# One-hot tiles of a token listing, laid out with the position innermost instead of the column

## The chip, the cores and the metric

The kernel runs on one core of a Trainium2 chip. TensorE (PE) multiplies matrices, with weight loads shown apart as PEld; VectorE (DVE) and ScalarE (ACT) work on rows of the 128 partitions; GpSimd (POOL) does some elementwise work and issues indirect DMAs; SyncE (SP) issues the other DMAs. The metric is the device time of one execution in microseconds.

## What is computed

```python
x = fft(fft(x, axis=1), axis=2).real            # 8 x 3072 x 256 -> 24576 tokens of 256
h = x @ w_in                                    # 256 -> 2048
x = where(h > 0, h, exp(min(h, 0)) - 1) @ w_out # 2048 -> 256
logits = x @ w_gate                             # 8 experts, room for 3072 tokens each
for idx in argsort(-logits.flatten()):          # greedy, best logit first
    tok, e = idx // 8, idx % 8
    if assigned[tok] < 0 and counts[e] < 3072:
        assigned[tok] = e; counts[e] += 1
for e in range(8):
    out[assigned == e] = relu(x[assigned == e] @ w1[e]) @ w2[e]
```

## The kernel before

The first part, `moe1` (up to about 2000 us), does the transforms and the dense layer, and leaves the tokens in DRAM and the logits in the tile L. The second part, `moe2`, is where the change lies. It makes three kinds of work and interleaves them:

- `select(i)` finds which expert fills up next and at which logit (a bisection of 32 steps, each with a count on DVE and ACT and a small matmul), and gives every token of that expert a rank from 0 to 3071 in the tile ui, with 192 columns (token 128 j + p stands in column j of partition p).
- `listing(i)` turns the ranks into a list of token numbers. It splits a rank into rb, its last seven bits, and qb, the rest (0 to 23). The columns are taken 16 at a time, in 12 chunks. For a chunk DVE builds `oh`, for each of the 16 columns the one-hot of rb (128 wide, L479), and `oq`, 48 wide: the one-hot of qb scaled by the partition number in its upper half (L473, scaled on ACT at L475), and by the column number in its lower half (L474). `place` (L452) then multiplies, for each of the 16 columns, oh as the weights with oq as 48 moving columns, 16 matmuls into one PSUM tile. DVE adds that tile to pj (L457, the first chunk L459). For expert 0, before any expert runs, oh and oq live in other buffers (yh, yl, hh.., hl..), L474 runs on POOL, and all chunks add up in one PSUM tile. At the end idx (L498) is computed from pj and the tokens are fetched by indirect DMA (yg, L522).
- `expert(i)` runs six groups of 512 tokens. In each, eight steps of six 512-column matmuls (L553) into the three buffers of hps, each followed by a relu on ACT (hh, L565) and the rounding rest on DVE (hl, L571), which frees the buffer; then transposes of the next group (`turn`, L531, L534, L535), then 96 matmuls of 256 columns (L594 to L596).

The interleaving is fixed when the program is built: a small clock model in the kernel counts estimated time on PE, DVE and ACT (`pe`, `dve`, `act`) and puts a piece of `listing` or `select` between two expert matmuls when DVE's estimated time is not too far ahead. A chunk is counted there as 750 + 1300 ns of DVE and no time of PE, in the kernel before and in the changed one. On the chip each engine then works through its queue in that order. So that the lists are ready in time, `listing(i + 1)` runs during `expert(i)`; there are 84 chunks in seven such bursts, and 12 chunks of expert 0 in a start-up before the first expert. While the listing runs, POOL also computes the rounding rests of the next expert's weights (w1l at L434, w2l at L440), two-input subtractions of 1024 elements.

Of the kernel before, what the change touches and what calls it, by code (L numbers as in the profile page):

```python
# [11 lines left out]
BF16 = mybir.dt.bfloat16  # L12
I32 = mybir.dt.int32
U16 = mybir.dt.uint16
AF = mybir.ActivationFunctionType
OP = mybir.AluOpType
# [145 lines left out]
def moe2(tc, yd, R, w1, w2, out):  # L162
    nc = tc.nc
    L, kh, kl, hm, mx, eq = (R[n] for n in ("L", "kh", "kl", "hm", "mx", "eq"))
    identf, identb, jp = R["identf"], R["identb"], R["jp"]
    iof, pci, pe8, es2, esn = (R[n] for n in ("iof", "pci", "pe8", "es2", "esn"))
    from contextlib import ExitStack
    with ExitStack() as ctx:
        con = ctx.enter_context(tc.tile_pool(name="con2", bufs=1))
        ctx.enter_context(nc.allow_low_precision(reason="counts up to 2048 are exact in float16"))  # L170
        rt = ctx.enter_context(tc.tile_pool(name="rt", bufs=1))
        wp = ctx.enter_context(tc.tile_pool(name="wp", bufs=1))
        ex = ctx.enter_context(tc.tile_pool(name="ex", bufs=2))
# [4 lines left out]
        def rps(shape, dtype=F32):  # L178
            return psum.tile(shape, dtype, name="rps")

        pcol = con.tile([128, 1], F32, name="pcol")
        tri = con.tile([128, 128], BF16, name="tri")
        onesb = con.tile([128, NJ], BF16, name="onesb")
        io16 = con.tile([128, 128, 16], BF16, name="io16")
        jb = con.tile([128, NJ], BF16, name="jb")
        trij = con.tile([96, 2, NJ], BF16, name="trij")
        pc96 = con.tile([128, 1], F32, name="pc96")
# [8 lines left out]
        def consts():  # L196
            nc.gpsimd.memset(asg, 0.0)
            nc.vector.tensor_scalar(tri, jp, 0.0, None, op0=OP.is_gt)
            nc.vector.memset(onesb, 1.0)
            yield  # L200
            nc.vector.tensor_copy(pcol, pci)
            nc.vector.tensor_copy(jb, iof)
            yield
            nc.vector.tensor_scalar(pc96, pcol, 96.0, None, op0=OP.add)
            nc.vector.tensor_scalar(em8, iof[:, 0:E], -8.0, None, op0=OP.add)
            yield
            nc.vector.tensor_scalar(pd8i, pci, 3, None, op0=OP.logical_shift_right)
            nc.vector.tensor_scalar(pe7, pe8, -8.0, None, op0=OP.add)
            nc.vector.tensor_copy(pd8, pd8i)
            yield  # L210
            nc.vector.tensor_scalar(wsel, iof[:, 0:16], pd8, 100.0, op0=OP.not_equal, op1=OP.mult)
            nc.vector.tensor_scalar(wsel, wsel, pe7, None, op0=OP.add)
            for h in range(2):
                yield
                nc.vector.tensor_scalar(trij[:, h], iof[0:96], (pcol, pc96)[h][0:96], None, op0=OP.is_gt)
            for h in range(4):
                yield
                hs = slice(32 * h, 32 * h + 32)
                nc.vector.tensor_copy(io16[:, hs], iof[:, hs].unsqueeze(2).to_broadcast([128, 32, 16]))

        setup = consts()
        NT = NC * 128

        def small(name, w=1, dtype=F32, bufs=2):
            return rt.tile([128, w], dtype, name=name, bufs=bufs)
# [20 lines left out]
        def act(d):  # L246
            ck.act = max(ck.act, ck.pe + 200) + d

        def dve(d, after=0):
            ck.dve = max(ck.dve, ck.pe + 200, after) + d  # L250
# [3 lines left out]
        def after():  # L254
            return max(ck.dve, ck.act) + AF0
# [157 lines left out]
        def listing(i):  # L413
            while i not in st:
                yield None
            rb, qb, wix = (st[i][n] for n in ("rb", "qb", "wix"))
            wr = [wp.tile([128, 2 * FE], F32, name="wr%d" % a) for a in range(2)]
            for a, src in enumerate((w1.rearrange("e (p c) f -> (e p) (c f)", c=2),
                                     w2.rearrange("e (p c) d -> (e p) (c d)", c=8))):
                nc.gpsimd.indirect_dma_start(out=wr[a], out_offset=None, in_=src,  # L420
                                             in_offset=bass.IndirectOffsetOnAxis(ap=wix[:, 0:1], axis=0))
            fetched = ck.pe
            pj = small("pj", 48)
            prev = None
            while now[0] < i - 1:
                yield None
            wsp = [wp.tile([128, 2 * FE], F32R, name=n, bufs=2) for n in ("w1h", "w1l", "w2h", "w2l")]

            def split():
                for c in range(2):  # L430
                    rv = wr[0].rearrange("p (c f k) -> p c k f", c=2, k=8)[:, c]
                    hv, lv = (t.rearrange("p (c k f) -> p c k f", c=2, k=8)[:, c] for t in wsp[0:2])
                    nc.scalar.activation(hv, rv, AF.Copy)
                    (nc.gpsimd if i else nc.vector).tensor_tensor(lv, rv, hv, op=OP.subtract)  # L434
                    act(950)
                    yield after()
                for c in range(2):
                    ws = slice(1024 * c, 1024 * c + 1024)
                    nc.scalar.activation(wsp[2][:, ws], wr[1][:, ws], AF.Copy)
                    nc.gpsimd.tensor_tensor(wsp[3][:, ws], wr[1][:, ws], wsp[2][:, ws], op=OP.subtract)  # L440
                    act(950)
                    yield after()

            parts = split()

            if i == 0:
                pl0 = psum.tile([128, 48], F32, name="acc20")

            def place(c, oh, oq):
                pl = rps([128, 48]) if i else pl0  # L450
                for j in range(16):
                    nc.tensor.matmul(pl, oh[:, :, j], oq[:, :, j], start=j == 0 and (i > 0 or c == 0),  # L452
                                     stop=j == 15 and (i > 0 or c == NC - 1))
                if i == 0:
                    return
                if c:
                    nc.vector.tensor_tensor(pj, pl, pj, op=OP.add)  # L457
                else:
                    nc.vector.tensor_copy(pj, pl)  # L459

            for c in range(NC):
                js = slice(16 * c, 16 * c + 16)
                if i:
                    oh = rt.tile([128, 128, 16], BF16, name="oh", bufs=2)
                    oq = rt.tile([128, 48, 16], BF16, name="oq", bufs=2)
                else:
                    oh = ex.tile([128, 128, 16], BF16, name=("yh", "yl")[c % 2])
                    oq = ex.tile([128, 48, 16], BF16, name="h%s%d" % ("hl"[c % 2], c // 2), bufs=1)

                def row(a, n):  # L470
                    return a[:, js].unsqueeze(1).to_broadcast([128, n, 16])

                nc.vector.tensor_tensor(oq[:, 24:48], io16[:, 0:24], row(qb, 24), op=OP.is_equal)  # L473
                (nc.vector if i > 0 else nc.gpsimd).tensor_tensor(oq[:, 0:24], oq[:, 24:48], row(jb, 24), op=OP.mult)  # L474
                nc.scalar.activation(oq[:, 24:48], oq[:, 24:48], AF.Copy, scale=pcol)  # L475
                dve(750)
                act(450)
                yield 0
                nc.vector.tensor_tensor(oh, io16, row(rb, 128), op=OP.is_equal)  # L479
                if prev:  # L480
                    place(*prev)
                prev = (c, oh, oq)
                dve(1300)
                if ck.pe > fetched + WAIT:
                    next(parts, None)
                yield after()
            place(*prev)
            while ck.pe < fetched + WAIT and i and not draining[0]:
                yield None
            if i:  # L490
                yield from parts
            st[i]["listed"] = True
            while now[0] < i - 1:
                yield None
            idx = small("idx", 24, I32)
            if i == 0:
                nc.vector.tensor_copy(pj, pl0)
            nc.vector.scalar_tensor_tensor(idx, pj[:, 0:24], 128.0, pj[:, 24:48], op0=OP.mult, op1=OP.add)  # L498
            plan[i] = dict(idx=idx, wr=wr)
            plan[i]["w"] = wsp  # L500
            if i:
                ahead()
            else:
                fetch(*queue.pop(0))
                out_y[0] += 1
            dve(100)
            yield after()
            yield from parts
# [4 lines left out]
        def ahead():  # L513
            while queue and out_y[0] < 3 and queue[0][0] in plan:
                fetch(*queue.pop(0))
                out_y[0] += 1
# [116 lines left out]

        sel_s = Stream(select, E)
        lst_s = Stream(listing, E)

        def ready(i):
# [655 lines left out]
```

## Time and profile before

| What | Value |
|---|---|
| Median of 3 runs | 3498.51 us (3496.53 to 3498.52) |
| The profiled execution, its own time | 3501.21 us |
| Its span, first to last instruction | 3499.4 us |
| PE busy over the span | 3343.9 us (96%) |
| DVE busy over the span | 2637.1 us (75%) |
| Mean granted TensorE clock | 0.974 of full speed |

Busy time is the time in which an engine works on an instruction; a busy PE may still be slowed, since a matmul's own duration overlaps that of the next. What a matmul costs is read from the distance between starts.

### The profile page before, as it was taken

What the parts mean: (1) busy time and instruction counts of PE and PEld (TensorE: products, weight loads), DVE (VectorE), ACT (ScalarE), POOL (GpSimd) and SP (SyncE); (2) the same over time, 40 slices, a digit from 0 to 9 for tenths busy, and PEclk for the clock granted to TensorE, in tenths of its full rate; (3) what the DMA queues carried; (4) which work ended last, traced back from release to release, by engine and by line L of the source; (5) the groups of instructions that cost most, each with busy time, mean ns of one, the idle gap of its engine ahead of it and who ended that gap; (6) DMA issues with size and microseconds to landing.
All of it is one profiled execution on the core that took longest, in us unless ns stands there. A gap on an engine that the chain in (4) does not pass through costs nothing.

```text
span 3499.4 us, 62303 instructions
## 1 busy us (share of the span) xinstructions
PE 3343.9 (96%) x25464; PEld 3121.6 (89%) x25464; DVE 2637.1 (75%) x4924; ACT 2253.9 (64%) x3029; POOL 649.7 (19%) x836
## 2 busy tenths in 40 slices
PE   7999999999999999999999838999999999999998
PEld 4999999999999999999999827888798888888997
DVE  7887888888878888888878887677677777767432
ACT  3787777778778777777777636454546464545332
POOL 5000000000000000000000033333343434343332
PEclk9999999999999999999999958999999999999999
DMA  7112121121121121211100001111111111111110
GB/s 196 35 45 52 41 45 31 51 42 40 32 45 51 34 44 40 42 46 36 37 13 13 19 25 43 49 48 51 40 55 44 53 43 60 63 36 61 40 46 31
DMA packets 97078, 159.30 MB, mean 46 GB/s; under 512 B 18464, under 2 KB 68632, under 8 KB 94616
## 3 DMA queue, kind: packets, MB, share of 16 engines
q1 hardware_dynamic: 67016, 64.05, 7.4%
q0 software_dynamic: 24576, 80.21, 7.4%
q10 hardware_dynamic: 5200, 11.05, 1.1%
q8 instruction: 200, 3.28, 0.4%
q14 instruction: 86, 0.70, 0.1%
HBM read 91.78 MB, written 63.47 MB: 44 GB/s over the span
## 4 chain that ended last, share of the span: by engine, by line
PE 85%; DVE 6%; ACT 4%; issue 2%; DMA 1%; POOL 0%; another core or an unknown queue 0%; ACTq 0%; DVEq 0%; POOLq 0%
PE hps L553 14%; PE acc L1113 11%; PE acc L1112 11%; PE acc L1114 11%; PE pq L1059 5%; PE pq L1061 5%; PE pq L1060 5%; PE acc L594 4%; PE acc L595 4%; PE acc L596 4%; PE rps L452 3%; PE pq L1063 3%; ACT junk L289 3%; PE pq L786 2%; PE pq L865 1%
## 5 line engine op out<-in xcount | busy, mean ns | idle before, releaser
L1114 PE MATMUL acc<-woh,gl 128*128 128x264 f32 x3072 | 872.8, 284 | 1.4 <-DVE gl L1099 1.4
L1113 PE MATMUL acc<-wol,gh 128*128 128x264 f32 x3072 | 874.0, 285 | 0.0
L1112 PE MATMUL acc<-woh,gh 128*128 128x264 f32 x3072 | 873.0, 284 | 1.0 <-DVE wol L1033 1.0
L1114 PEld LDWEIGHTS acc<-woh,gl 128*128 128x128 f32 x3072 | 578.0, 188 | 1.9 <-DVE gl L1099 1.8
L1112 PEld LDWEIGHTS acc<-woh,gh 128*128 128x128 f32 x3072 | 578.5, 188 | 1.2 <-issue 1.2
L1113 PEld LDWEIGHTS acc<-wol,gh 128*128 128x128 f32 x3072 | 577.6, 188 | 0.0
L1082 ACT ACTIVATE e<-h 128x1024 f32<-128x1024 f32 x384 | 407.7, 1062 | 158.8 <-DVE h L1076 158.8
L1075 DVE TENSOR_TENSOR h<-pq,qs 128x512 f32<-128x512 f32 x384 | 265.5, 691 | 284.9 <-ACT qs L1069 284.0
L1099 DVE TENSOR_TENSOR gl<-g,gh 128x1024 fp32r<-128x1024 f32 x384 | 467.5, 1217 | 1.6 <-ACT gh L1094 1.6
L1089 DVE SCALAR_TENSOR_TENSOR g<-e,h 128x1024 f32<-128x1024 f32 x384 | 466.9, 1216 | 0.1
L594 PE MATMUL acc<-w2h,hh 128*128 128x256 f32 x1536 | 456.6, 297 | 0.0
L595 PE MATMUL acc<-w2l,hh 128*128 128x256 f32 x1536 | 436.2, 284 | 0.0
L596 PE MATMUL acc<-w2h,hl 128*128 128x256 f32 x1536 | 435.6, 284 | 0.0
L571 DVE SCALAR_TENSOR_TENSOR hl<-hps,hh 128x512 fp32r<-128x512 f32 x384 | 262.7, 688 | 217.1 <-ACT hh L565 202.7
L1084 ACT ACTIVATE e<-e 128x1024 f32<-128x1024 f32 x384 | 407.3, 1061 | 10.7
L1094 ACT ACTIVATE gh<-g 128x1024 fp32r<-128x1024 f32 x384 | 403.6, 1051 | 2.1 <-PE acc L1113 2.1
L1069 ACT ACTIVATE qs<-pq 128x512 f32<-128x512 f32 x384 | 229.8, 598 | 208.2 <-PE pq L1063 204.3
L565 ACT ACTIVATE hh<-hps 128x512 fp32r<-128x512 f32 x384 | 226.5, 593 | 198.8 <-PE hps L553 157.6
L604 POOL DMA_INDIRECT out<-osb,yg x192 | 201.9, 1052 | 619.5 <-ACT osb L601 587.2
L553 PE MATMUL hps<-yh,w1h 128*128 128x512 f32 x768 | 312.7, 407 | 2.0 <-DVE hl L571 1.8
L553 PE MATMUL hps<-yh,w1l 128*128 128x512 f32 x768 | 303.1, 395 | 0.0
L553 PE MATMUL hps<-yl,w1h 128*128 128x512 f32 x768 | 301.9, 393 | 0.0
(318 smaller groups left out, 7477.8 us busy)
## 6 DMA issues: line engine op xcount, KB each, us to landing
yd<-ysb SPq DMA_DIRECT2D x48, 514.0 KB
zd<-zev SPq DMA_DIRECT2D x30, 385.5 KB
xa<-x SPq DMA_DIRECT2D x28, 384.0 KB
zt<-zd SPq DMA_DIRECT2D x16, 193.5 KB
xa<-w_out ACTq DMA_DIRECT2D x6, 512.0 KB
zt<-zd SPq DMA_DIRECT2D x32, 96.0 KB
yg<-yd,idx POOLq DMA_INDIRECT x192
out<-osb,yg POOLq DMA_INDIRECT x192
```

What stands on the lines that cost most here:

```text
L553: nc.tensor.matmul(ps, w[:, ws], v[:, c], start=c + k == 0, stop=c + k == 3)
L594: nc.tensor.matmul(acc[t // 2][:, t % 2], hh[:, ts], w2h[:, fs], start=f == 0, stop=False)
L595: nc.tensor.matmul(acc[t // 2][:, t % 2], hh[:, ts], w2l[:, fs], start=False, stop=False)
L596: nc.tensor.matmul(acc[t // 2][:, t % 2], hl[:, ts], w2h[:, fs], start=False, stop=f == 7)
L1082: nc.scalar.activation(e, st["h"], AF.Relu, scale=-1.0)
L1084: nc.scalar.activation(st["e"], st["e"], AF.Exp, scale=-1.0)
L1089: nc.vector.scalar_tensor_tensor(g, st["e"], -1.0, st["h"], op0=OP.add, op1=OP.max)
L1094: nc.scalar.activation(st["gh"], st["g"], AF.Copy)
L1099: nc.vector.tensor_tensor(st["gl"], st["g"], st["gh"], op=OP.subtract)
L1112: nc.tensor.matmul(o, st["gh"][:, i, ts], woh(c), start=c == 0, stop=False)
L1113: nc.tensor.matmul(o, st["gh"][:, i, ts], wol(c), start=False, stop=False)
L1114: nc.tensor.matmul(o, st["gl"][:, i, ts], woh(c), start=False, stop=c == 15)
```

## The change

All one-hot tiles are turned: where the column index of a chunk (16) was the innermost dimension, the position (128 or 48) now is. So `oh[:, j]` and `oq[:, j]`, which a matmul reads, are 128 and 48 neighbouring elements, where before they lay 16 elements apart. On the DVE side, `row` now spreads each rank over the innermost dimension (a step of zero there), where before it repeated a row of 16 ranks. The constant io16 is turned in the same way. The counts of elements stay.

```diff
-        io16 = con.tile([128, 128, 16], BF16, name="io16")
+        io16 = con.tile([128, 16, 128], BF16, name="io16")
...
-                hs = slice(32 * h, 32 * h + 32)
-                nc.vector.tensor_copy(io16[:, hs], iof[:, hs].unsqueeze(2).to_broadcast([128, 32, 16]))
+                hs = slice(4 * h, 4 * h + 4)
+                nc.vector.tensor_copy(io16[:, hs], iof[:, 0:128].unsqueeze(1).to_broadcast([128, 4, 128]))
...
-                    nc.tensor.matmul(pl, oh[:, :, j], oq[:, :, j], start=j == 0 and (i > 0 or c == 0),
+                    nc.tensor.matmul(pl, oh[:, j], oq[:, j], start=j == 0 and (i > 0 or c == 0),
...
-                    oh = rt.tile([128, 128, 16], BF16, name="oh", bufs=2)
-                    oq = rt.tile([128, 48, 16], BF16, name="oq", bufs=2)
+                    oh = rt.tile([128, 16, 128], BF16, name="oh", bufs=2)
+                    oq = rt.tile([128, 16, 48], BF16, name="oq", bufs=2)
...
-                    return a[:, js].unsqueeze(1).to_broadcast([128, n, 16])
-
-                nc.vector.tensor_tensor(oq[:, 24:48], io16[:, 0:24], row(qb, 24), op=OP.is_equal)
-                (nc.vector if i > 0 else nc.gpsimd).tensor_tensor(oq[:, 0:24], oq[:, 24:48], row(jb, 24), op=OP.mult)
-                nc.scalar.activation(oq[:, 24:48], oq[:, 24:48], AF.Copy, scale=pcol)
+                    return a[:, js].unsqueeze(2).to_broadcast([128, 16, n])
+
+                nc.vector.tensor_tensor(oq[:, :, 24:48], io16[:, :, 0:24], row(qb, 24), op=OP.is_equal)
+                (nc.vector if i > 0 else nc.gpsimd).tensor_tensor(oq[:, :, 0:24], oq[:, :, 24:48], row(jb, 24), op=OP.mult)
+                nc.scalar.activation(oq[:, :, 24:48], oq[:, :, 24:48], AF.Copy, scale=pcol)
```

No instruction is added, removed or moved: every engine's queue has the same instructions in the same order as before; only the shapes and steps of L219, L452, L473, L474, L475 and L479 differ.

## Rows read from the trace of the kernel before

**Rows 1.** The page: busy us of each engine; the chain that ended last.
```profile
PE 3343.9 (96%) x25464; PEld 3121.6 (89%) x25464; DVE 2637.1 (75%) x4924; ACT 2253.9 (64%) x3029; POOL 649.7 (19%) x836
...
PE 85%; DVE 6%; ACT 4%; issue 2%; DMA 1%; POOL 0%; another core or an unknown queue 0%; ACTq 0%; DVEq 0%; POOLq 0%
```

**Rows 2.** Timeline of PE, one placement; start us, duration us, what.
```profile
3264.42 1.73 PE L452 MATMUL rps<-oq,oh 128*128 128x48 bf16 x16
3265.94 0.36 PE L594 MATMUL acc<-w2h,hh 128*128 128x256 f32 x1
```

**Rows 3.** Timeline of PE, twelve matmuls with contiguous bf16 operands.
```profile
2378.97 0.44 PE L342 MATMUL rps<-wb,gm 128*128 128x16 bf16 x12
2379.27 0.47 PE L553 MATMUL hps<-yh,w1h 128*128 128x512 f32 x1
```

**Rows 4.** Timeline of DVE, one chunk between two placements.
```profile
3266.32 0.35 DVE L473 TENSOR_TENSOR oq<-io,qb 128x384 bf16<-128x384 bf16 x1
3266.70 0.36 DVE L474 TENSOR_TENSOR oq<-oq,jb 128x384 bf16<-128x384 bf16 x1
3266.98 1.22 DVE L479 TENSOR_TENSOR oh<-io,rb 128x2048 bf16<-128x2048 bf16 x1
3270.63 0.21 DVE L457 TENSOR_TENSOR pj<-rps,pj 128x48 f32<-128x48 f32 x1 [2.43 <-PE rps L452]
```

**Rows 5.** Instructions of lines 409, 405, 264 and 219: ns min/median/max, first and last start.
```profile
L409 DVE TENSOR_TENSOR asg<-asg,u x8: 357/357/360, 2102.3 to 3231.5; 128x192 f32<-128x192 f32 x8
L405 DVE TENSOR_TENSOR L<-L,cc x7: 1748/1750/1751, 2276.5 to 3218.2; 128x1536 f32<-128x1536 f32 x7
L264 DVE TENSOR_TENSOR eq<-L,mx x7: 1757/1758/3852, 2108.6 to 3089.9; 128x1536 bf16<-128x1536 f32 x7
L219 DVE CAST io<-iof x4: 417/417/418, 2014.5 to 2020.1; 128x512 bf16<-128x512 f32 x4
```

**Rows 6.** Start-up, all engines: one cycle of two chunks.
```profile
2094.96 1.21 DVE L479 TENSOR_TENSOR yh<-io,rb 128x2048 bf16<-128x2048 bf16 x1
2095.12 1.85 POOL L474 TENSOR_TENSOR hh<-hh,jb 128x384 bf16<-128x384 bf16 x1 [0.29 <-DVE hh L473]
...
2096.10 1.07 DVE L473 TENSOR_TENSOR hl<-io,qb 128x384 bf16<-128x384 bf16 x1
...
2097.10 1.21 DVE L479 TENSOR_TENSOR yl<-io,rb 128x2048 bf16<-128x2048 bf16 x1
```

**Rows 7.** Busy time by stretch, from a burst's first placement to its last: PE, PEld, DVE, ACT, POOL.
```profile
2220.00:2276.00 56.00, 54.83 (x415) 49.63 (x413) 34.76 (x57) 22.39 (x32) 19.85 (x19) 0.97 0.06 21
...
3221.00:3279.00 58.00, 58.00 (x464) 53.88 (x463) 38.25 (x60) 23.30 (x32) 28.24 (x27) 1.00 0.20 67
sum 443.00, PE 439.67 PEld 400.98 DVE 305.76 ACT 183.58 POOL 185.94; mean PE 62.81 PEld 57.28 DVE 43.68 ACT 26.23 POOL 26.56
```

**Rows 8.** The same stretches, L479 alone: busy us and count, clock, DMA share.
```profile
2220.00:2276.00 56.00, 13.58 (x12) 0.97 0.06 21
...
3221.00:3279.00 58.00, 13.39 (x11) 1.00 0.20 67
```

**Rows 9.** Timeline, two subtractions on POOL and DVE beside them.
```profile
3239.24 3.06 POOL L434 TENSOR_TENSOR w1l<-wr,w1h 128x1024 fp32r<-128x1024 f32 x1
...
3240.32 4.55 DVE L473 TENSOR_TENSOR oq<-io,qb 128x384 bf16<-128x384 bf16 x1
...
3242.25 2.40 POOL L440 TENSOR_TENSOR w2l<-wr,w2h 128x1024 fp32r<-128x1024 f32 x1
```

**Rows 10.** Groups by line from 2114 us on: count, busy us, mean ns, idle before.
```profile
L479 DVE TENSOR_TENSOR oh<-io,rb 128x2048 bf16<-128x2048 bf16 x84 | 106.6, 1269 | 0.0
...
L473 DVE TENSOR_TENSOR oq<-io,qb 128x384 bf16<-128x384 bf16 x84 | 54.7, 651 | 0.2
...
L474 DVE TENSOR_TENSOR oq<-oq,jb 128x384 bf16<-128x384 bf16 x84 | 32.9, 391 | 2.9
```

More of the change, by code (lines that the diff above doesn't have):

```diff
@@ L463, in listing @@
                 if i:
-                    oh = rt.tile([128, 128, 16], BF16, name="oh", bufs=2)
-                    oq = rt.tile([128, 48, 16], BF16, name="oq", bufs=2)
-                else:
-                    oh = ex.tile([128, 128, 16], BF16, name=("yh", "yl")[c % 2])
-                    oq = ex.tile([128, 48, 16], BF16, name="h%s%d" % ("hl"[c % 2], c // 2), bufs=1)
+                    oh = rt.tile([128, 16, 128], BF16, name="oh", bufs=2)
+                    oq = rt.tile([128, 16, 48], BF16, name="oq", bufs=2)
+                else:
+                    oh = ex.tile([128, 16, 128], BF16, name=("yh", "yl")[c % 2])
+                    oq = ex.tile([128, 16, 48], BF16, name="h%s%d" % ("hl"[c % 2], c // 2), bufs=1)
                 def row(a, n):
-                    return a[:, js].unsqueeze(1).to_broadcast([128, n, 16])
-                nc.vector.tensor_tensor(oq[:, 24:48], io16[:, 0:24], row(qb, 24), op=OP.is_equal)
-                (nc.vector if i > 0 else nc.gpsimd).tensor_tensor(oq[:, 0:24], oq[:, 24:48], row(jb, 24), op=OP.mult)
-                nc.scalar.activation(oq[:, 24:48], oq[:, 24:48], AF.Copy, scale=pcol)
+                    return a[:, js].unsqueeze(2).to_broadcast([128, 16, n])
+                nc.vector.tensor_tensor(oq[:, :, 24:48], io16[:, :, 0:24], row(qb, 24), op=OP.is_equal)
+                (nc.vector if i > 0 else nc.gpsimd).tensor_tensor(oq[:, :, 0:24], oq[:, :, 24:48], row(jb, 24), op=OP.mult)
+                nc.scalar.activation(oq[:, :, 24:48], oq[:, :, 24:48], AF.Copy, scale=pcol)
                 dve(750)
```

## The prediction

> **What bounds the kernel now.** I read the page first. PE is busy 96% of the span and carries 85% of the chain that ended last, DVE only 75% [rows 1]. That reads as if whatever shortens PE shortens the kernel. But the change touches PE in seven bursts, so the share that matters is the one inside them. The view by stretch gives it: from a burst's first placement to its last the seven make 443 us, in which PE is busy 439.7 and DVE 305.8, 69% [rows 7]. PE is the bound there, with 137 us of DVE idle beside it.
>
> Then the timelines. A placement of 16 matmuls starts at 3264.42 and the next matmul starts at 3265.94: 1.52 us of PE, 95 ns each [rows 2]. The twelve matmuls of L342, whose bf16 weights and moving columns are contiguous, take 2379.27 - 2378.97 = 0.30 us, 25 ns each [rows 3]. On DVE a chunk is 0.35 + 0.36 + 1.22 us and the addition to pj [rows 4].
>
> The start-up is another case: PE waits there, and DVE and POOL take turns. L479 runs from 2094.96 to 2096.17; L474 on POOL, started at 2095.12, ends only at 2096.97, 0.8 us after L479; the next L473, 0.35 us elsewhere, takes 1.07 and ends just after that. A chunk takes 2097.10 - 2094.96 = 2.14 us, all of it in this ring [rows 6].
>
> **PE's side of the change.** With both operands contiguous I take the rate of L342 and a little for 48 instead of 16 columns: 16 x 28 ns = 0.45 us a placement. Gain 1.52 - 0.45 = 1.07 us, times 84 = 90 us of PE. The bounds are 0 (if the distance of elements is not what costs) and 16 x 25 ns, a gain of 94 us.
>
> **DVE's side.** L479 does 2048 elements in 1.22 us. L405, two fp32 inputs, needs 1.75 us for 1536, L409 0.36 us for 192: 1.04 ns an element over a fixed part [rows 5]. So L479 now goes at two elements in the time of one there. The bf16 operands it reads and writes are all neighbours; with the change the second input stands still along the innermost dimension. No row has bf16 operands of that kind. Lower bound: the rate stays, 1.22 us. Upper bound: one element at a time, 1.75 + 512 x 0.00104 = 2.28 us. For the lower speaks L219, which reads a value that stands still 16 times and yet does 512 elements in 417 ns; it has one input. For the upper speaks L264, which has two inputs, one of them standing still, and takes 1.76 us for 1536, as L405 does [rows 5]; it is fp32. Two inputs is the closer kin, so I take the upper: L479 +1.06 us, and L473 and L474 with 384 elements 0.36 + 192 x 0.00104 = 0.56 us, +0.21 and +0.20. A chunk costs DVE 1.47 us more, 84 chunks 123.5 us.
>
> The Trainium skill (Vector Engine (DVE) Microarchitecture Reference, 5.1 Performance modes) says that a two-source operation with 2-byte operands, one of which read a single element 16 times over, ran at one element a cycle. By that rule the upper end holds, 123.5 us; by L219's rate nothing is added. No run here shows it yet.
>
> **Where these meet.** Within the 443 us PE would need 443 - 90 = 353. DVE has 78 of the 84 chunks in those stretches (the view of L479 alone counts 12 in the first and 11 in each of the six others [rows 8]; the others' DVE part lies just ahead, in idle time): 305.8 + 78 x 1.47 = 420.5 us. So DVE becomes the bound of the bursts. That is the main step: a gain of 90 on PE is cut to at most 443 - 420.5 = 22.5.
>
> To this comes POOL. An L473 of 0.35 us took 4.55 because it stood until two subtractions on POOL had ended [rows 9], and POOL stood for L479 in the start-up [rows 6]: two-input work of DVE and POOL excludes each other. The three lines were busy 106.6 + 54.7 + 32.9 = 194.2 us [rows 10], at 84 x (1.22 + 0.35 + 0.36) = 162.1 unhindered [rows 4], so they were held for 32 us; much of POOL's work fell in DVE's idle time, such as the 2.43 us before an addition to pj [rows 4]. That idle time is what the change uses up. If holds grow with the time that DVE spends in such work, (194.2 + 123.5) / 194.2 = 1.64, they become 53 us, 21 more. Bounds: 0, and about 45 if DVE is held for nearly all of POOL's subtractions. With 21 the bursts need 441.5 us of DVE. Nor is DVE ever wholly busy, since it still waits for ACT at each turn of a group; I allow 1 us a burst, an estimate, 7 us. Sum: 448.5 against 443, **+5 us**, with the bounds 420.5 (-22) and 441.5 - 21 + 45 + 7 = 472.5 (+30).
>
> **Start-up.** The ring is L479, POOL's 0.8, and the rest of L473. L479 grows by 1.06 and L473 by 0.21, nothing hides it: 12 x 1.27 = 15.2. Only the last placement is on the path, -1.07. **+14 us**. If POOL needs longer for L474 in its new shape (no row shows it), up to its 0.8 us again, 12 x 0.8 = 10 more; with unchanged DVE rates it is -1.
>
> **Free edits.** ACT's L475 keeps its 384 elements and ACT is busy 184 of the 443 us [rows 7]; io16 is filled by four copies of as many elements as before (417 ns each [rows 5]), at worst, at one element a cycle, 4 x 0.3 = 1 us. The queues' order is the same, so no wait is added by it. What is late when DVE lags is hl, which frees the hps buffers that L553 needs, and oh, for which L452 waits.
>
> The sum, against the profiled execution's own 3501.2: +14 +5 = 3520. The median of the runs shown is 2.7 lower, so 3517.
>
> **Rivals.**
>
> 1. DVE keeps two elements at a time (L219's rate). Then DVE adds nothing, PE's 90 us come off and the start-up gains 1: 3498.5 - 91 = 3408. For it speaks L219 alone; against it L264. Chance 0.07.
>
> 2. Not slower: DVE lags, but the holds don't grow, because POOL's subtractions still fall beside hl and pj, which read PSUM and were not held. Then the bursts take DVE's bare 420.5, -22, and the start-up +14: 3498.5 - 8 = 3490. It decides at about 14 us: if the holds and leftover waits of the bursts together add less than 22.5 - 14 = 8 us, the kernel is not slower. For it: the idle time of 137 us is large, and the lag at a burst's end is paid back in the 4 us or so before the last placement. Chance 0.22, over 3478 to 3503.
>
> 3. The matmuls don't get faster: then only DVE's side is left. Bursts that were bound by PE at 443 must also take 441.5 to 448.5 of DVE with less room for either to run ahead; with some 10 to 20 us lost to that and +14, 3525 to 3540. Against it: 25 ns at L342. The Trainium skill (TensorE: Matmul & The Clock Gate, Weight-path perf modes) says that the fast weight load takes packed or strided columns alike. By that rule the weights' layout would give nothing, and only the moving columns could. The trace can't part the two in the placement. Chance 0.08.
>
> 4. PE, which now stands often, loses clock. The burst with a stop of about a microsecond had a granted clock of 0.97, the last one, with none, 1.00 [rows 7]. Three per cent of 443 us is 13 more: 3530. Chance 0.10.
>
> The forecast itself, 3500 to 3535, has 0.53.
>
> **Numbers.** A measurement of this kernel can tell about 0.2%, 7 us. Faster: rival 1, and 0.16 of rival 2: 0.23. Same: the rest of rival 2 and 0.06 of the forecast, 0.12. Slower: 0.65. The range leaves out rival 1 and the ends: from 3475, rival 2 with some lag carried out of the bursts, to 3550, the upper bound of the holds (+30) with the start-up's +14 and part of POOL's 10.
>
> **What would show it.** L479 at 2.28 us and L473, L474 at 0.56; placements at 0.45 us of PE; the seven stretches at 440 to 455 us with DVE busy above 95% and PE idle there by 80 us or more, before L452 and L553, released by oh and hl; a start-up cycle of 3.4 us; L473 and L479 held for 50 us or more. The prediction is wrong if L479 stays at 1.2 us, if the placements stay at 1.5, or if the stretches shrink to 425 with DVE busy throughout.

## The result, and the profile after

The changed kernel takes 3540.11 us, median of 4 runs (3537.72 to 3540.16), against 3498.52 before (4 runs): a ratio of 1.011, interval 1.0098 to 1.0122, 41.6 us slower. The forecast was 3517, 18.5 us slower. The direction held, and 3540 lies inside the outer range (3475 to 3550); it lies above the band of 3500 to 3535 to which the forecast itself gave 0.53, and the size was less than half of the real one.

The page's first lines for the changed kernel: busy us of each engine, and the shares of the chain that ended last.

```profile
PE 3280.0 (93%) x25464; PEld 3039.9 (86%) x25464; DVE 2776.4 (78%) x4924; ACT 2253.3 (64%) x3029; POOL 703.6 (20%) x836
...
PE 74%; DVE 17%; ACT 4%; issue 2%; DMA 1%; POOL 1%; another core or an unknown queue 0%; ACTq 0%; DVEq 0%; SPq 0%; POOLq 0%
```

PE works 64 us less than in [rows 1] and the kernel is longer; DVE's share of the chain has gone from 6% to 17%. The prices of the single instructions came out as forecast. First DVE: the view of L479 and of L473 (ns min/median/max).

```profile
L479 DVE TENSOR_TENSOR oh<-io,rb x84: 2274/2284/4386, 2230.4 to 3313.8; 128x2048 bf16<-128x2048 bf16 x84
L473 DVE TENSOR_TENSOR oq<-io,qb x84: 543/551/4842, 2229.4 to 3312.7; 128x384 bf16<-128x384 bf16 x84
```

2.284 us where 2.28 was forecast, 0.551 where 0.56 was. Then PE, the timeline of one placement:

```profile
2938.90 0.58 PE L452 MATMUL rps<-oq,oh 128*128 128x48 bf16 x16
2939.32 0.36 PE L594 MATMUL acc<-w2h,hh 128*128 128x256 f32 x1
```

16 matmuls take 0.42 us, 26 ns each, where [rows 2] had 1.52 and the forecast 0.45. Over 84 placements that is 92 us of PE saved. And the start-up, one cycle:

```profile
2105.21 2.28 DVE L479 TENSOR_TENSOR yh<-io,rb 128x2048 bf16<-128x2048 bf16 x1
2105.37 2.81 POOL L474 TENSOR_TENSOR hh<-hh,jb 128x384 bf16<-128x384 bf16 x1 [0.49 <-DVE hh L473]
...
2107.41 1.18 DVE L473 TENSOR_TENSOR hl<-io,qb 128x384 bf16<-128x384 bf16 x1
...
2108.51 2.28 DVE L479 TENSOR_TENSOR yl<-io,rb 128x2048 bf16<-128x2048 bf16 x1
```

A cycle is 3.30 us (forecast 3.4; 2.14 in [rows 6]). From the first L473 of listing(0) to the first L553 it is 57.45 us, before 44.3: +13.1, forecast +14.

What is left of the span's +39.0 us (3538.4 against 3499.4) lies behind the first L553: 1412.5 us against 1385.0, +27.4 where +5 was forecast; the work ahead of the start-up came out 1.6 shorter. Busy time by stretch, from a burst's first placement to its last (PE, PEld, DVE, ACT, POOL, granted clock, DMA share, GB/s):

```profile
2232.80:2283.60 50.80, 41.99 (x411) 35.10 (x411) 49.68 (x56) 21.58 (x31) 26.83 (x19) 1.00 0.06 22
...
2751.20:2824.50 73.30, 61.62 (x502) 52.84 (x501) 64.31 (x75) 26.60 (x39) 30.62 (x23) 0.88 0.08 25
...
sum 458.60, PE 379.87 PEld 325.75 DVE 417.96 ACT 179.01 POOL 221.27; mean PE 54.27 PEld 46.54 DVE 59.71 ACT 25.57 POOL 31.61
```

The stretches of [rows 7] were rounded outward by 3 us; measured as here, the kernel before gives:

```profile
sum 440.00, PE 436.84 PEld 399.01 DVE 303.00 ACT 182.77 POOL 184.49; mean PE 62.41 PEld 57.00 DVE 43.29 ACT 26.11 POOL 26.36
```

So the bursts cost +18.6, and what lies between them the other 9. In the sum, 79 us of PE and 41 us of DVE stand idle: neither engine fills the stretch. In the first burst DVE is indeed full (49.7 of 50.8), and that one got shorter, 50.8 against 56.0. The six others have DVE at 88 to 94%, and a granted clock of 0.88 to 0.93 (before 0.98 to 1.00).

Who waits for whom from the first burst to the last, 2232 to 3319 us (us in all, times, longest us):

```profile
DVE hl L571 <- ACT hh L565: 41.5, 96, 1.5
PE hps L553 <- DVE hl L571: 26.2, 15, 8.2
PE rps L452 <- DVE pj L457: 20.6, 12, 3.6
PE rps L271 <- DVE pj L457: 16.1, 5, 5.4
```

PE waits for DVE, as forecast. DVE in turn waits for hh, which ACT makes from what PE has just finished, and within the seven bursts these waits of L571 make 22 us. The longest stop shows the whole pattern; timeline of all engines:

```profile
2952.07 7.23 DVE L264 TENSOR_TENSOR eq<-L,mx 128x1536 bf16<-128x1536 f32 x1
2952.53 2.86 POOL L434 TENSOR_TENSOR w1l<-wr,w1h 128x1024 fp32r<-128x1024 f32 x1
2955.33 2.34 POOL L440 TENSOR_TENSOR w2l<-wr,w2h 128x1024 fp32r<-128x1024 f32 x1
...
2959.22 1.28 DVE L571 SCALAR_TENSOR_TENSOR hl<-hps,hh 128x512 fp32r<-128x512 f32 x2
...
2959.96 0.79 PE L553 MATMUL hps<-yh,w1h 128*128 128x512 f32 x1 [8.17 <-DVE hl L571]
...
2962.79 0.69 DVE L571 SCALAR_TENSOR_TENSOR hl<-hps,hh 128x512 fp32r<-128x512 f32 x1 [1.23 <-ACT hh L565]
2963.10 0.63 PE L553 MATMUL hps<-yl,w1h 128*128 128x512 f32 x1
...
2963.52 0.63 PE L553 MATMUL hps<-yh,w1h 128*128 128x512 f32 x1
...
2964.34 0.39 PE L553 MATMUL hps<-yl,w1h 128*128 128x512 f32 x1
...
2964.57 0.39 PE L553 MATMUL hps<-yh,w1h 128*128 128x512 f32 x1
```

L264, 1.76 us alone, stands until both subtractions on POOL are over (2957.67) and ends 1.6 us after that; L571 is queued behind it, no hps buffer comes free, and PE stands for 8.17 us. Then, for 4.4 us, L553 starts every 420 to 430 ns, afterwards every 230. The stretches say the same in clock:

```profile
2959.90:2964.30 4.40, 4.34 (x24) 3.32 (x25) 3.14 (x6) 2.59 (x4) 1.83 (x4) 0.50 0.17 61
2964.30:2970.00 5.70, 5.70 (x44) 4.47 (x43) 4.87 (x8) 1.79 (x5) 4.79 (x4) 1.00 0.24 57
```

After the stop PE works at 0.50, the 1.2 GHz level, and then at 1.00, the 2.4 GHz level. While it is slow, hh comes later and DVE, the engine that was behind, waits too.

Holds, groups by line from 2114 us on (busy us, mean ns, idle before):

```profile
L479 DVE TENSOR_TENSOR oh<-io,rb 128x2048 bf16<-128x2048 bf16 x84 | 197.5, 2351 | 0.0
...
L473 DVE TENSOR_TENSOR oq<-io,qb 128x384 bf16<-128x384 bf16 x84 | 69.9, 832 | 0.2
...
L474 DVE TENSOR_TENSOR oq<-oq,jb 128x384 bf16<-128x384 bf16 x84 | 55.2, 657 | 2.9
...
L264 DVE TENSOR_TENSOR eq<-L,mx 128x1536 bf16<-128x1536 f32 x7 | 20.5, 2930 | 0.2
```

Unhindered the three lines would take 84 x (2.284 + 0.551 + 0.557) = 284.9 of their 322.6 us: held for 38 us, where the forecast had 53 and [rows 10] 32.

### The profile page after: what moved, and what is told of

Read it like the earlier page. It is cut to its first block, busy times and chain, and to the rows that moved or that the text cites. A ratio compares the mean times of both kernels' runs of the same rounds, so it can differ in the third digit from the quotient of the medians.

```text
span 3538.4 us, 62303 instructions
## 1 busy us (share of the span) xinstructions
PE 3280.0 (93%) x25464; PEld 3039.9 (86%) x25464; DVE 2776.4 (78%) x4924; ACT 2253.3 (64%) x3029; POOL 703.6 (20%) x836
## 4 chain that ended last, share of the span: by engine, by line
PE 74%; DVE 17%; ACT 4%; issue 2%; DMA 1%; POOL 1%; another core or an unknown queue 0%; ACTq 0%; DVEq 0%; SPq 0%; POOLq 0%
PE hps L553 11%; PE acc L1113 10%; PE acc L1112 10%; PE acc L1114 10%; PE pq L1059 5%; PE pq L1061 5%; PE pq L1060 5%; DVE oh L479 4%; ACT junk L289 3%; PE pq L1063 3%; PE acc L594 2%; PE acc L596 2%; PE acc L595 2%; DVE oq L473 2%; DVE hl L571 2%
## 5 line engine op out<-in xcount | busy, mean ns | idle before, releaser
L1075 DVE TENSOR_TENSOR h<-pq,qs 128x512 f32<-128x512 f32 x384 | 265.6, 692 | 285.2 <-ACT qs L1069 284.3
L571 DVE SCALAR_TENSOR_TENSOR hl<-hps,hh 128x512 fp32r<-128x512 f32 x384 | 261.0, 687 | 184.8 <-ACT hh L565 171.0
L604 POOL DMA_INDIRECT out<-osb,yg x192 | 230.2, 1199 | 609.9 <-ACT osb L601 576.4
L553 PE MATMUL hps<-yh,w1h 128*128 128x512 f32 x768 | 319.6, 416 | 29.0 <-DVE hl L571 26.2
L596 PEld LDWEIGHTS acc<-w2h,hl 128*128 128x128 f32 x1536 | 299.6, 195 | 11.2 <-DVE hl L571 11.0
L553 PE MATMUL hps<-yh,w1l 128*128 128x512 f32 x768 | 307.5, 400 | 0.0
```

The costliest lines, as they stand in the source:

```text
L553: nc.tensor.matmul(ps, w[:, ws], v[:, c], start=c + k == 0, stop=c + k == 3)
L596: nc.tensor.matmul(acc[t // 2][:, t % 2], hl[:, ts], w2h[:, fs], start=False, stop=f == 7)
```

## The experiments

The first four ran on a chip where the kernel before takes 3500.4 us, the others on chips where it takes 3485.6 (e5 to e8) and 3485.4 (the rest), so ratios to the kernel before on the same chip are compared. The expectations count in us of a chip at 3500; for the others their ranges are to be read 0.4% lower. In e1 to e4, e8 and e10 the integer ranks qi share a buffer with another tile, to make room; e3 and e4 also have a second, small constant for oq. Bursts, from the first placement to the last, are given in a table behind the last experiment.

**1. The turned layout, with runs of two (e1_pairs).** Theory: L479 is slow because its second input stands still along the innermost dimension. If so, a rank that is kept twice, side by side, restores the rate, with the matmuls' operands as in the change.

```diff
-            rb = rt.tile([128, NJ], BF16, name="rb")
+            rb = rt.tile([128, NJ, 2], BF16, name="rb")      # qb, jb likewise
...
-                    return a[:, js].unsqueeze(2).to_broadcast([128, 16, n])
+                    return a[:, js].unsqueeze(2).to_broadcast([128, 16, n // 2, 2])
...
-                nc.vector.tensor_tensor(oh, io16, row(rb, 128), op=OP.is_equal)
+                nc.vector.tensor_tensor(two(oh), two(io16), row(rb, 128), op=OP.is_equal)
```

> The turned layout of the change, but each rank is kept twice side by side, so that the input that stood still along the innermost dimension now reads runs of two neighbours. Nothing is left out. If the loss comes from DVE's rate of one element at a time: L479 back at 1.22 us, L473 and L474 at 0.36, placements at 0.42 us of PE, the start-up cycle at 2.1 us, and nearly all of 84 x 1.09 = 92 us comes off the kernel before: 3405 to 3430. If the bursts are paced by other waits (the single PSUM tile of the placement, the fixed order), PE's gain turns into idle time: 3470 to 3500. If a run of two is not enough for the faster rate: as the change, 3535 to 3545.

3447.86, ratio 0.9851 (0.9834 to 0.9867). The view of its line for oh, a placement, and the bursts:

```profile
L483 DVE TENSOR_TENSOR oh<-io,rb x84: 1210/1218/3427, 2216.6 to 3224.2; 128x2048 bf16<-128x2048 bf16 x84
```
```profile
2401.99 0.58 PE L453 MATMUL rps<-oq,oh 128*128 128x48 bf16 x16
2402.41 0.48 PE L557 MATMUL hps<-yh,w1h 128*128 128x512 f32 x1
```
```profile
sum 389.10, PE 356.88 PEld 312.64 DVE 310.75 ACT 180.45 POOL 185.76; mean PE 50.98 PEld 44.66 DVE 44.39 ACT 25.78 POOL 26.54
```

The pair rate is back (1.218 us) with placements of 0.42, so the cause of DVE's price is shown. The Trainium skill (Vector Engine (DVE) Microarchitecture Reference, 5.1 Performance modes) says that a two-input operation yields two results a cycle when all its operands are 2 bytes wide and run over more than one neighbouring element innermost; the 1.218 us agree. But of PE's 92 us only 53 came back (3447.9 against 3500.4, about 2 of them in the start-up, 42.4 against 44.3), and the time lies between the first expectation (up to 3430) and the second (from 3470): here too, with DVE needing only 311 us, the bursts last 32 us longer than PE's work. That was the first sign that the forecast's 7 us for unfilled time was the weak term.

**2. DVE's side alone (e2_dve_alone).** The layout of before, but ranks in fp32, which cost DVE the pair rate.

```diff
-            rb = rt.tile([128, NJ], BF16, name="rb")
+            rb = rt.tile([128, NJ], F32, name="rb")          # qb, jb likewise
```

> The layout of before, with ranks in fp32, so that DVE pays its price (L479 2.28 us, L473 and L474 0.56) and PE gains nothing (placements 1.5 us). If DVE's work sets the time of the bursts, this is at least as slow as the change, since PE has 92 us more to do: 3540 to 3560. If what hurts in the change is that PE stands and then runs at the lower clock, PE stands less here, the clock stays near 0.97, and it is less slow than the change: 3515 to 3535.

3562.35, ratio 1.0177 (1.016 to 1.0194): L479 2.284 us, placements 1.52, so this is DVE's price without PE's gain, 2 us above the first expectation. Of its 62 us 15 are the start-up (59.4 against 44.3) and 45 the bursts:

```profile
sum 485.20, PE 451.33 PEld 407.19 DVE 424.06 ACT 182.87 POOL 221.86; mean PE 64.48 PEld 58.17 DVE 60.58 ACT 26.12 POOL 31.69
```

PE is the busier engine here, and still 34 us are unfilled. So DVE's slower rate is dear by itself, and beside it PE's 92 us are worth only 62 - 41.6 = 20 us.

**3 and 4. One operand at a time (e3_weights_only, e4_columns_only).** In e3 only oh is turned, in e4 only oq; the other tile keeps the layout of before.

```diff
-                    nc.tensor.matmul(pl, oh[:, j], oq[:, j],
+                    nc.tensor.matmul(pl, oh[:, j], oq[:, :, j],      # e3
+                    nc.tensor.matmul(pl, oh[:, :, j], oq[:, j],      # e4
```

> Only oh, the weights, is turned; oq, the moving columns, keeps the layout of before. If the distance between weights cost PE its time, the placement is at 0.42 us, DVE pays 1.06 us a chunk, and the time is a little under the change's: 3510 to 3530. If the moving columns cost it, the placement stays near 1.5 us and the time is near that of e2 less 84 x 0.4 us: 3530 to 3550.

> Only oq, the moving columns, is turned; oh keeps the layout of before. DVE pays 0.41 us a chunk. If the moving columns cost PE its time, the placement is at 0.42 us, and 92 us less of PE against 34 us more of DVE leave 3425 to 3450. If the weights cost it, the placement stays at 1.5 us and the time is 3500 to 3515.

e3: 3536.37, ratio 1.0106 (1.0089 to 1.0122). e4: 3490.32 (10 runs), ratio 0.9971 (0.9961 to 0.998). Timelines of a placement, e3 and then e4:

```profile
2402.69 1.58 PE L454 MATMUL rps<-oq,oh 128*128 128x48 bf16 x16
2404.05 0.36 PE L599 MATMUL acc<-w2h,hh 128*128 128x256 f32 x1
```
```profile
2399.11 1.17 PE L454 MATMUL rps<-oq,oh 128*128 128x48 bf16 x16
2400.12 0.36 PE L599 MATMUL acc<-w2h,hh 128*128 128x256 f32 x1
```

The starts within a placement lie, in the median, 89 ns apart with strided columns, 62 with strided weights, 97 with both, 25 with neither. Each stride costs by itself, and the slower of the two nearly sets the pace. So in e4 neither expectation is right (placement 1.01 us), and in e3, whose time fits the second, the placement is 1.36 us and not 1.5. e4, which pays only the small part of DVE's price, is 0.3% faster than the kernel before; e3 is as slow as the change, with 55 us more of PE's work in its bursts. The Trainium skill's "packed or strided" (TensorE: Matmul & The Clock Gate, Weight-path perf modes) isn't borne out as a statement of time here: a bf16 weight tile with 32 bytes between elements comes every 62 ns, a contiguous one every 25.

**5. The change without POOL's subtractions (e5_no_rests).**

```diff
...
-                    (nc.gpsimd if i else nc.vector).tensor_tensor(lv, rv, hv, op=OP.subtract)
+                    if i == 0:
+                        nc.vector.tensor_tensor(lv, rv, hv, op=OP.subtract)    # L440 likewise
```

> The change, without POOL's (and no one's) subtractions L434 and L440 for experts 1 to 7: these use expert 0's rounding rests, so that part of the weights is left out of the result. If DVE being held by POOL makes the long stops of PE (8.2 us once, before an L264 that two subtractions held), the 46 us of holds go, PE's stops fall from 80 to 30 us, its clock in the bursts returns to 0.97 or more: 3490 to 3510. If DVE's own work sets the pace, only a part of the holds shows: 3520 to 3535.

3469.13, ratio 0.9949 (0.9933 to 0.9966); below the expected range even scaled to this chip. The view of its line for oh, and the bursts:

```profile
L482 DVE TENSOR_TENSOR oh<-io,rb x84: 2276/2284/2328, 2225.3 to 3243.6; 128x2048 bf16<-128x2048 bf16 x84
```
```profile
sum 402.80, PE 357.83 PEld 309.04 DVE 368.54 ACT 178.38 POOL 139.12; mean PE 51.12 PEld 44.15 DVE 52.65 ACT 25.48 POOL 19.87
```

No L479 is held any more (longest 2328 ns), DVE is busy 49 us less and the bursts are 56 us shorter. PE does the same matmuls in 358 instead of 380 us: with fewer stops it kept its clock (0.97 to 1.00 in each burst).

**Its control: the kernel before without them (c1_before_no_rests)**, the same edit.

> The control to e5: the kernel before without the subtractions L434 and L440 for experts 1 to 7 (expert 0's rounding rests are used, so that part of the weights is left out). If holds by POOL cost the kernel before little, because they fall in DVE's idle time (32 us of holds, 7 us of PE's stops in the bursts), this is 0 to 12 us faster than before, and most of the 72 us that e5 gained is a cost which the change brought about. If they cost it as much as the change, it is 50 us or more faster.

3480.09 (10 runs), ratio 0.9983 (0.9973 to 0.9993): 0.17%, about 6 us.

```profile
sum 433.70, PE 433.19 PEld 396.64 DVE 265.62 ACT 183.52 POOL 102.06; mean PE 61.88 PEld 56.66 DVE 37.95 ACT 26.22 POOL 14.58
```

Here DVE is busy 303.0 - 265.6 = 37 us less, and the bursts are only 6 us shorter. So POOL's holds existed before, in DVE's idle time, at nearly no price; the change makes them grow by only 12 us (49 against 37), but it takes away the idle time, and the same subtractions then cost 1.6% (1.011 against 0.9949), some 55 us.

**6. The addition to pj ahead of L479 (e6_pj_first).** PE's waits before L452 and L271 end with L457, which frees the one PSUM tile of a placement and is queued behind L479.

```diff
-                nc.vector.tensor_tensor(oh, io16, row(rb, 128), op=OP.is_equal)
                 if prev:
                     place(*prev)
+                nc.vector.tensor_tensor(oh, io16, row(rb, 128), op=OP.is_equal)
```

> The change, with the addition to pj queued on DVE ahead of the next L479 instead of behind it, so that the one PSUM tile, for which the next placement and select's matmuls wait, comes free 2.2 us earlier. If that tile is what PE stands for (43 us of its stops ended with pj), 25 to 40 us come off: 3500 to 3515. If DVE's total work decides, DVE now waits for PE there and the time stays: 3530 to 3550.

3517.27, ratio 1.0085 (1.0069 to 1.0102): on this chip the lower end of the second expectation, and not clear of the change's 1.011 (1.0098 to 1.0122). PE's waits for pj fell from 37 us to 6, but those for hl rose from 26 to 36 and 23 appeared for oh; PE's idle time in the bursts stayed at 79 us. The stop is moved, not removed.

**7. The planner told of the price (e7_planner_told).**

```diff
-                dve(750)
+                dve(1150)
...
-                dve(1300)
+                dve(2400)
```

> The change, with the clock model told DVE's new cost of a chunk (1150 + 2400 instead of 750 + 1300 ns), so that the chunks are spread further apart. If the stops come from an order made for the old cost, PE's stops in the bursts halve and the clock stays up: 3495 to 3520. If DVE's work is too much for the expert's time wherever it stands, the stops move to the end of each expert, where the list must be ready: 3530 to 3560.

3614.19, ratio 1.0368 (1.0351 to 1.0385). PE's waits from 2232 to 3400 us:

```profile
PE rps L452 <- DVE pj L457: 78.2, 31, 4.9
PE hps L553 <- DVE hl L571: 39.1, 25, 3.9
PE tps L531 <- DMA yg<-yd,idx: 37.3, 23, 4.4
```

A planner that counts more DVE time per chunk places fewer of them beside the matmuls; the rest runs one after the other at the end of the expert, where PE has nothing beside it (in the fourth burst the last four placements follow each other from 2852.4 to 2868.3 with no other matmul between), and the lists and their fetches come late. The second expectation was right in kind and too small.

**8. Runs of two, and pj ahead (e8_pairs_pj)**, e1 with the edit of e6.

> The version of e1 (ranks kept twice) with pj queued ahead of L479. If the PSUM tile is what PE still stands for in e1, its 36 us of idle time in the bursts halve: 3425 to 3438. If the holds by POOL and hl are, it stays: 3443 to 3452.

3426.75, ratio 0.9826 (0.981 to 0.9843): the best version by its median, 1.7% under the kernel before and 2.8% under the change, but not clear of e1 (0.9834 to 0.9867). The bursts take 383 us, 6 less than in e1, and PE's idle time in them is 30 us against 32: it didn't halve. As in e6, waits for pj went and others came: in the bursts 14.6 us before L453 and L271 became 3.5, while those for hl rose from 15.7 to 19.3 and 6.6 appeared for oh.

**9 and 10. The subtractions on DVE (e9_rests_on_dve, e10_pairs_pj_dve), with the kernel before as control (c2_before_dve).** Is it the long holds, or DVE's time as such? On DVE the subtractions hold nothing, and take DVE's time in its own order.

```diff
-                    (nc.gpsimd if i else nc.vector).tensor_tensor(lv, rv, hv, op=OP.subtract)
+                    nc.vector.tensor_tensor(lv, rv, hv, op=OP.subtract)    # L440 likewise for i > 0
```

> The change, with the subtractions L434 and L440 of experts 1 to 7 on DVE instead of POOL: DVE gets 28 x 1.22 = 34 us of work in its own order and loses 46 us of holds. If what hurts is the long stretch in which DVE stands for POOL, and PE then for DVE, at a lower clock afterwards, 25 to 50 us come off: 1.1% slower than before becomes 0.4% faster to 0.4% slower. If only DVE's total time counts, 12 us at most come off: 0.7 to 1.1% slower than before.

> The version of e8 (ranks kept twice, pj first) with these subtractions on DVE too. DVE was busy 310 of 383 us in its bursts, 36 of it holds. If the holds are behind the 34 us of PE's idle time that are left there, 10 to 25 us come off e8: 2.0 to 2.4% faster than before. If DVE becomes too busy: 1.3 to 1.7% faster.

> The control to e9: the kernel before with these subtractions on DVE. If holds cost it little, the 34 us more of DVE work are hidden or cost a little: 0.2% faster to 0.4% slower than before.

e9: 3516.38, ratio 1.0091 (1.0074 to 1.0108), not clear of the change, the second expectation. e10: 3431.86, 0.9847 (0.983 to 0.9863), no better than e8, in the range for a DVE that becomes too busy, though DVE is no busier than in e8 (307 us against 310). c2: 3500.27, 1.0045 (1.0028 to 1.0062), just outside its expectation. The bursts of e9:

```profile
sum 453.90, PE 378.91 PEld 324.37 DVE 412.72 ACT 179.46 POOL 142.22; mean PE 54.13 PEld 46.34 DVE 58.96 ACT 25.64 POOL 20.32
```

With 413 us of DVE and L479 and L264 never held (longest 2.33 and 1.76 us), the bursts last 454 us, nearly as in the change. The exchange was nearly even: on DVE an L440 takes 1.21 us but an L434 2.06, so the 28 subtractions are 46 us and not 34, against 49 us of holds that e5 took away. So it isn't the length of single holds that costs; it is DVE's time, whoever takes it. Its place in the queue counts beside it: in c2 DVE is busy only 6 us more than before and the bursts are 14 us longer, with PE waiting 11.5 us for hl in L553, where it waited 1.8 before.

The bursts of all kernels (us, worked out from the views by stretch), and what is left above the busier of the two engines:

| Kernel | length | PE | DVE | less over busier | above the busier |
|---|---|---|---|---|---|
| c1, before without subtractions | 433.7 | 433.2 | 265.6 | 0.61 | 0.5 |
| before | 440.0 | 436.8 | 303.0 | 0.69 | 3 |
| c2, before, subtractions on DVE | 454.3 | 442.5 | 309.2 | 0.70 | 12 |
| e4, columns only | 428.3 | 400.8 | 345.4 | 0.86 | 28 |
| e10, pairs, pj ahead, subtractions on DVE | 388.8 | 356.7 | 306.8 | 0.86 | 32 |
| e1, pairs | 389.1 | 356.9 | 310.8 | 0.87 | 32 |
| e7, planner told | 478.3 | 357.8 | 409.8 | 0.87 | 69 |
| e8, pairs, pj ahead | 382.9 | 353.0 | 309.9 | 0.88 | 30 |
| e6, pj ahead | 452.7 | 374.1 | 421.5 | 0.89 | 31 |
| e3, weights only | 461.9 | 435.4 | 391.3 | 0.90 | 27 |
| after | 458.6 | 379.9 | 418.0 | 0.91 | 41 |
| e9, subtractions on DVE | 453.9 | 378.9 | 412.7 | 0.92 | 41 |
| e2, DVE alone | 485.2 | 451.3 | 424.1 | 0.94 | 34 |
| e5, no subtractions | 402.8 | 357.8 | 368.5 | 0.97 | 34 |

## Why the prediction was right in direction and wrong in size

**PE's gain** was right: 1.09 us a placement for 1.07. That both operands' strides cost, each by itself, is shown by e3 and e4.

**DVE's price** was right, and by its cause (e1): L479 2.284 for 2.28, L473 and L474 0.55 for 0.56. The choice of L264 over L219 came out right, but L264 couldn't carry it: L405, in which both inputs run over neighbours, takes the same 1.75 us in fp32 [rows 5], so L264's 1.76 says nothing of an input that stands still. That the choice held was in part luck; that an input which stands still is the cause, e1 shows. Rival 1 (the pair rate stays) and rival 3 (the matmuls don't get faster) are out.

**The start-up** was right, +13.1 for +14.

**Where the missing time lies.** In the profiled executions the forecast was +19 us and the span grew by 39. Of the 20 us between them 14 lie in the bursts (+18.6 for +5) and 9 between them, which the prediction put at nothing without a reason; the start-up and the work ahead of it came out 1 and 2 us lower.

**Where these meet** was right in kind: DVE becomes the busier engine of the bursts and PE's 92 us turn into 79 us of standing. **The step that failed is the sum behind it.** It put DVE at 441.5 us in the bursts and added "1 us a burst, an estimate, 7 us" for the time in which DVE isn't busy: 448.5 in all. Measured: DVE 418.0, idle 40.6, together 458.6. Two terms were off in opposite ways. The holds were put at +21 and are +12 (49 us in the change by e5, 37 before by c1), and the bare growth, 368.5 - 265.6 = 103 us, is less than 78 x 1.47 = 115, since the durations of successive instructions overlap by a little and 77 chunks, not 78, lie in the measured stretches. (The 2.43 us of [rows 4], given as DVE's idle time with POOL's work in it, has no subtraction: POOL only issued transfers there, L604.) The idle allowance was 7 and should have been 41. What it named, the turns of a group (L535 waiting for ACT's L534), came to 3 us in the seven bursts; what it left out came to 31: L571 waiting for hh, 22 us, and select's L273 waiting for the transposes of L271, 9 us. This decided the size, and that the sum came within 10 us of 458.6 is in part luck, since DVE's 441.5 was 24 too high. The table shows that the error isn't particular to the change: in the versions in which the less busy engine has 0.86 or more of the busier one's time, 27 to 41 us of the bursts are filled by neither (69 in e7, whose order is another), and at 0.70 and below 12 or less. No version lies between, and the versions differ in more than this ratio, so it is a finding of this kernel and not a rule that was tested. The forecast took the second kind of number, that of the kernel before, into a kernel of the first kind.

**Rival 4**, the lost clock, was given as an alternative at 13 us. It is a part of the case: PE's matmuls take 380 us in the bursts of the change and 358 in those of e5, 22 us more of the same work, and the longest stop shows how (0.50 of the clock for 4.4 us). How much of DVE's 41 us of idle time comes from it, and how much would be left at full clock, no run isolates; e5, with a clock of 0.97 to 1.00, still has 34 us unfilled, so the clock isn't the main part of it.

**Rival 2**, not slower because the holds don't grow, named a point of 8 us for holds and leftover waits; these came to 12 and 41. It is out; on the holds the truth lay between it (no growth) and the forecast (21).

**What would show it**: the stretches are 459 us, not 440 to 455; DVE is busy 91% of them, not above 95%; the holds of the three lines are 38 us, not 50 or more; and L452 waits for pj (the PSUM tile, 20.6 us), not for oh (1.8 us in the view of L479). The last matters little: e6 takes that wait away, and another takes its place.

**Open**: the 9 us between the bursts. Of them about 6 are PE's idle time outside the bursts (36.2 against 30.0 us from the first L553 to PE's last matmul). They weren't traced further, and the time outside the bursts also differs from chip to chip (945 to 949 us in e1 to e4, 930 to 938 in the later runs except e7, here 945.0 before and 953.9 after). On two chips the versions with the change's DVE rate stand 2 to 6 us above those without it (e9 934.5 against 930 to 932 in c1, c2 and e10; e5 and e6 937.5 against 932.0 in e8), on the third the difference is 1 us (e2 949.4, e1 948.6). So how much of the 9 us is the change's own isn't settled.

## What to carry to other kernels

Before turning a tile so that TensorE reads neighbours, look at the instruction that writes it: if one of the two 2-byte inputs then stands still along the innermost dimension, DVE pays nearly twice (2.284 us for 1.218 here); keeping that input in pairs gives both engines what they want (1.011 becomes 0.9851). When a change brings two engines that feed each other near to one another, don't take the larger of their sums as the time: in this kernel, at 0.86 and more of one another, 27 to 41 us of some 400 were filled by neither, and 69 in one order. And idle time of an engine off the path may be paying for another engine's work (POOL's subtractions: 0.17% while DVE had room, 1.6% without), so ask who lives in it before it is spent.

## What the runs showed of the hardware

- A bf16 matmul of 48 columns starts every 25 ns with contiguous operands, every 62 with weights 32 bytes apart, every 89 with moving columns 32 bytes apart, every 97 with both.
- An instruction on DVE with two inputs stood through two successive subtractions on POOL (7.23 us instead of 1.76), without getting its turn between them, although its record starts 0.46 us before the first of them. The Trainium skill (SBUF — State Buffer, Who interferes with whom) says that a DVE instruction with two SBUF inputs contends with a GpSimd instruction that reads SBUF, and that the shared ports are an exclusive lock; the trace agrees, and adds that the engine that stands can lose twice in a row.
- In the start-up L474 on POOL, 1.85 us in [rows 6], took 2.81: it stands for L479 as before and ends 0.7 us after it (2108.18 against 2107.49), so the new shape costs POOL nothing that the kernel pays for.
